# Attention through 32 packed rows, then a squared-ReLU layer: the first batch's second softmax and first layer in two token groups, another order of the transposed keys, one transpose for the left-over tokens, and a new order of the work

## The chip, the cores and the metric

The kernel runs on one core of a Trainium2 chip. The metric is the device time of one execution in microseconds (us). A core has a matrix engine (TensorE, "PE" in the profile; its loads of the stationary operand are listed apart as "PEld"), a vector engine (VectorE, "DVE"), an activation engine (ScalarE, "ACT"), a general engine (GpSimd, "POOL") and an engine that only starts transfers here (SyncE, "SP"). Each engine works off its own queue in the order in which the program put its instructions there; between engines, semaphores make one wait for another. Matrix products land in PSUM, which has eight banks of 512 fp32 values for each of 128 partitions; the other engines read them there and write to SBUF.

## What is computed

```python
def _attn_ref(q, k, v, p):            # q, k, v: 8 batches, 8 heads, 576 tokens, 64; p: 8, 8, 32, 64
    def sm_attn(qq, kk, vv):          # softmax(qq kk^T / 8) vv
        ...
    p_packed = sm_attn(p, k, v)                 # 32 rows for each head: over 576 keys
    return sm_attn(q, p_packed, p_packed)       # 576 rows for each head: over 32 keys

def _moe_ref(x, w_in, w_out):         # x: 4608 tokens x 512, w_in: 512 x 2048, w_out: 2048 x 512
    r = np.maximum(x @ w_in, 0.0)
    return (r * r) @ w_out
```

The first softmax packs each head's keys and values into 32 rows; the second attends from each token to these 32 rows; the heads side by side are x, which goes through two dense layers with a squared ReLU between them. Matrix products run in bf16.

## The kernel before, in words

**Tiles and stages.** The work of a batch b goes through named steps; the names below are those of the code, and the text keeps to them.

- Loads: `Lk`, `Lq` (two each, four heads in one), `Lv` (two), for the weights `LWI` (eight) and `LWO` (eight; number c brings the blocks 2c and 2c+1 of w_out). All are issued on POOL's queue, at most eight unfinished at a time (`dq`), in the order of the list `ld` (lines 790 to 797).
- `Tk`, `Tq` (lines 387 to 396): DVE's 32x32 transposes bring keys and queries into the layout with the head's dimension on the partitions. Row a*18+j of a head lies in partition a, so that the transposed tensor has the order j*32+a.
- `S1` (line 398): scores of the 32 packed rows against 576 keys, two steps for a batch (four heads in each), then maximum (DVE), exponential (ACT) and division (DVE). The values come in another order than the keys, so S1 writes its scores with `main = ps.rearrange("p (g i a j2) -> p i g j2 a")`: neighbouring columns of the product go to every second fp32 value of the PSUM bank. It takes four products of 256 columns and two of 64.
- `E` (line 426): five PE transposes of the weights, and a copy from PSUM. `PV` (line 436): product with the values, 20 small products for each of two steps. `XT`: eight small copies (`pq_block`) and one (`extract`) put the packed rows into `pq_bd` (block diagonal, for S2) and `ppT` (for M).
- `M` (line 464): since x is a product with the packed rows, the first layer's weights are multiplied with them beforehand: M = packed rows times w_in, four chunks of 512 columns.
- `S2` (lines 486 to 535): scores of 576 tokens against 8 x 32 rows. Four token tiles of 128 go into a pair of PSUM banks (16 products), the last 64 tokens into another bank (4 products). DVE takes maximum and difference, ACT the exponential, DVE sum, reciprocal and product. Batch 0 (`SOLO`) does this in three parts (512, 512 and 128 columns), the other batches in one chain `C` of 1152 columns.
- `N` (lines 537 to 549): PE transposes of the result, one step for each half of the heads: four of 128 tokens and, for the last 64 tokens, one whose operand has 64 partitions only (line 544); then one copy of 576 columns.
- `F1` (lines 553 to 579): 16 blocks of 128 of the first layer's 2048 outputs. A step is four products of 288 columns, a ReLU from PSUM into a buffer `r` (four buffers; for batch 0 in two halves that ACT and DVE may share, `SPLIT`), and a square into `gT`, which holds two batches.
- `F2` (lines 583 to 596): for each of 36 tiles of 128 output tokens, 16 products of 512 columns that add up in one PSUM bank, a copy to SBUF and four transfers out on SP's queue. The tiles with even and with odd numbers are two streams, each with one of two banks at a time. Step F2.t.fb needs block fb of the batches that the tile's tokens come from: tiles 0 to 3 lie in batch 0, tile 4 in batches 0 and 1.

**Order.** The program is written by a planner (`Plan`, lines 50 to 227): every step has engines, estimated durations, dependences, PSUM banks and buffers; a list schedule with priorities (`TABLE`, line 230, and `levels`) decides in which order the instructions go into each engine's queue, and which of two engines takes a piece with alternatives. The order is fixed when the program is built. In the first 70 us of the plan, where the planner expects PE to be idle by over 0.45 us, it puts products of a zero matrix ahead of the next step (`keep_clock`, line 302, and `fills`, line 220); they keep PE's clock up and compute nothing.

Of the kernel before, what the change touches and what calls it, by code (L numbers as in the profile page):

```python
# [14 lines left out]
P = 128  # L15
# [34 lines left out]
class Plan:  # L50
# [179 lines left out]
TABLE = {'o': {'X.0': 10.65, 'X.1': 31.58, 'S1.5': 9.41, 'S1.3': -12.52, 'S1.6': -24.93, 'F1.5': 1.74, 'F2.11': 5.6,  # L230
    'N.0': -2.17, 'N.1': -5.48, 'N.2': -15.81, 'N.3': -0.5, 'N.4': -3.15, 'N.5': 4.81, 'N.6': 5.79, 'N.7': 3.42,
    'XT.7': -5.75, 'E.0': 1.99, 'E.1': 1.31, 'E.2': -4.89, 'E.3': -1.37, 'E.4': -8.69, 'E.5': 7.0, 'E.6': 13.74,
    'E.7': 23.02, 'F1.0': -1.88, 'F1.1': -3.45, 'F1.2': -8.22, 'F1.3': -8.4, 'F1.4': -16.3, 'F1.6': 2.12, 'F1.7':
    -14.31, 'P.0': -2.78, 'PV.1': 0.87, 'Tk.5': 8.92, 'M.3': -7.32, 'S1.1': -12.25, 'F2.14': -6.87, 'Tk.3': -0.35,
    'Tq.3': 4.31, 'PV.3': -9.68, 'XT.3': 1.16, 'S2.3': -17.72, 'C.3': -1.2, 'Tk.6': 6.64, 'Tq.6': 46.24, 'PV.6':
    -6.38, 'XT.6': 0.8, 'M.6': 28.77, 'S2.6': -11.88, 'C.6': 19.91, 'XT.4': -14.43, 'I2': -11.49, 'F2.28': 16.93,
    'F2.23': -1.98, 'C.4': -17.29, 'XT.1': -8.34, 'Tq.7': 23.72, 'PV.0': -7.15, 'PV.2': 10.69, 'PV.4': -27.42, 'PV.5':
    -11.67, 'PV.7': 3.53, 'P.2': -15.62, 'XT.5': -13.02, 'M.0': 10.82, 'M.1': 4.52, 'M.2': 10.51, 'M.4': 2.36, 'M.5':
    21.31, 'M.7': 25.09, 'Tk.7': 3.83, 'S1.7': -6.54, 'S2.7': -10.25, 'C.7': 22.2, 'Tq.2': 3.39, 'C.2': -42.42,
    'Tk.4': 26.02, 'Tq.4': 10.05, 'S1.4': -17.0, 'S2.4': -24.58, 'F2.0': 15.91, 'F2.2': -4.29, 'F2.4': 10.23, 'F2.6':  # L240
    6.49, 'F2.8': 8.81, 'F2.10': 12.87, 'F2.12': 20.48, 'F2.16': -1.8, 'F2.18': -3.93, 'F2.20': 10.23, 'F2.22': 6.86,
    'F2.24': 10.11, 'F2.26': 5.69, 'F2.30': 4.43, 'F2.32': -10.27, 'F2.34': 3.66, 'F2.1': 29.8, 'F2.3': 9.19, 'F2.5':
    18.21, 'F2.7': 4.21, 'F2.9': 8.01, 'F2.13': 12.3, 'F2.15': 6.13, 'F2.17': 5.45, 'F2.19': 10.23, 'F2.21': 17.24,
    'F2.25': 7.73, 'F2.27': 6.33, 'F2.29': 7.94, 'F2.31': 6.74, 'F2.33': 14.02, 'F2.35': 19.06, 'Tk.1': -11.46,
    'Tq.1': 1.8, 'S2.1': -26.07, 'C.1': -4.19, 'XT.0': -1.06, 'XT.2': 3.17, 'Tk.2': 0.09, 'S1.2': -4.93, 'S2.2':
    -16.14, 'S2.5': -21.05, 'I': 14.34, 'S2.0': -39.93, 'Tk.0': 0.31, 'Tq.5': 21.62, 'C.5': 7.12, 'S1.0': -9.28,
    'Tq.0': 10.06}, 'l': {'M.0': -0.12, 'M.1': -0.11, 'M.2': -1.84, 'M.3': -0.4, 'M.4': 0.01, 'M.5': -0.79, 'M.6':
    -0.47, 'M.7': -0.5, 'F2.0': -1.53, 'F2.2': -1.2, 'F2.4': -0.22, 'F2.6': -0.74, 'F2.8': -0.4, 'F2.10': -1.53,
    'F2.12': -0.34, 'F2.14': 0.35, 'F2.16': 0.07, 'F2.18': -0.4, 'F2.20': -1.37, 'F2.22': -0.4, 'F2.24': -0.77,
    'F2.26': -1.27, 'F2.28': 0.83, 'F2.30': 0.34, 'F2.32': -0.28, 'F2.34': 1.29, 'F2.1': -0.39, 'F2.3': -0.26, 'F2.5':  # L250
    -0.4, 'F2.7': -0.19, 'F2.9': -0.4, 'F2.11': -0.11, 'F2.13': -3.08, 'F2.15': -0.18, 'F2.17': 0.97, 'F2.19': -0.4,
    'F2.21': -0.4, 'F2.23': 0.97, 'F2.25': 1.65, 'F2.27': -0.4, 'F2.29': -0.4, 'F2.31': -0.8, 'F2.33': 0.25, 'F2.35':
    -0.4, 'E.0': -0.9, 'N.0': 0.35, 'E.5': 1.01, 'XT.3': -0.99, 'N.2': -0.01, 'X.1': 0.09, 'E.7': -1.48, 'N.3': 1.83,
    'E.4': 0.32, 'XT.2': -0.61, 'N.4': 0.55, 'N.6': 0.47, 'N.5': -0.66, 'N.7': 0.73, 'X.0': 0.28, 'XT.5': -1.4,
    'XT.6': 0.52, 'E.1': 0.07, 'XT.1': -0.36, 'XT.7': 0.93, 'E.3': 0.02, 'E.2': -0.51}, 'w': 0, 'm': 1.42}


def kernel_impl(tc, q, k, v, p, w_in, w_out, out):
# [11 lines left out]
    NKQ, NV = 16, 5  # L270
    VX = JT // 2

    with ExitStack() as ctx:
# [6 lines left out]
        rpool = ctx.enter_context(tc.tile_pool(name="rpool", bufs=4))  # L280
# [95 lines left out]
        class Att:  # L376
# [16 lines left out]
            def tr_k(self, qd):  # L393
                nc.vector.transpose(  # L394
                    kT[:, qd].rearrange("p dh (j a) -> p j dh a", a=32),
                    self.t.k[qd][:].rearrange("p (j dh dl) -> p j dh dl", dh=2, dl=32))

            def s1(self, qd, u):
                ps = self.ps1[qd] = pair(u).rearrange("p c n -> p (c n)")[:, :S]
                kv = [kT[:, qd, dh].rearrange("p (j2 x a) -> p x j2 a", j2=2, a=32) for dh in range(2)]  # L400
                w = [pT_bd[:, self.b, qd, dh] for dh in range(2)]
                main = ps[:, :GM * P].rearrange("p (g i a j2) -> p i g j2 a", i=2, a=32, j2=2)
                rest = ps[:, GM * P:].rearrange("p (a j2) -> p j2 a", j2=2)
                for i in range(2):
                    for dh in range(2):
                        nc.tensor.matmul(main[:, i], lhsT=w[dh], rhs=kv[dh][:, i * GM:(i + 1) * GM],  # L406
                                         start=(dh == 0), stop=(dh == 1))
                for dh in range(2):
                    nc.tensor.matmul(rest, lhsT=w[dh], rhs=kv[dh][:, 2 * GM], start=(dh == 0), stop=(dh == 1))  # L409
# [84 lines left out]

            def s2_rest(self, u):
# [6 lines left out]
            def src2(self, x):  # L502
                s = self.ps2r if x == 2 else self.ps2[:, x] if x < 2 else self.ps2[:].rearrange("p c n -> p (c n)")
                return s.rearrange("p (g i) -> p g i", i=32)
# [32 lines left out]
            def s2_tr(self, qd, u):  # L537
                ps = self.pst[qd] = bank(u).bitcast(BF16)[:, :S]
                for tt in range(4):
                    g0 = tt * 8 + qd * QH  # L540
                    nc.tensor.transpose(ps[:, tt * P:(tt + 1) * P],  # L541
                                        self.n2[:, g0:g0 + QH].rearrange("p g i -> p (g i)"), ident[:])
                o = 64 * qd
                nc.tensor.transpose(ps[:, 4 * P:S], self.n2[o:o + 64, 32:36].rearrange("p g i -> p (g i)"),
                                    ident[o:o + 64, o:o + 64])

            def s2_out(self, qd, eng):
                self.tile_of("a2", att, [P, NQD, S], BF16)
                cast(eng, self.a2[:, qd], self.pst[qd])
# [11 lines left out]
        def new_r(a, fb):  # L561
            rr[a.b, fb] = Att.cols(rpool.tile([P, S], BF16, name="r"))
# [38 lines left out]
        OB = [(6,), (7,)]  # L601

        plan = Plan({"kqb": NKQ, "vb": NV, "r": 4, "osb": 3, "dq": 8}, 8)
# [5 lines left out]

        def gate(b, x):  # L610
            y = (b - 2) * NFB + GATE[x] if b > 1 else GATE1[x] if b else -1
            return [f"F1.{y // NFB}.{y % NFB}"] if y >= 0 else []
# [243 lines left out]
```

## Time and profile before

| | us |
|---|---|
| median of 3 runs | 284.8 |
| the three runs | 284.8, 284.81, 282.79 |
| the profiled execution | 282.2 |
| its span, first to last instruction | 280.4 |
| PE busy (of it the zero products of line 304) | 265.5 (21.2) |
| DVE busy | 195.7 |
| ACT busy | 162.2 |
| POOL busy | 46.4 |
| TensorE clock granted | 1.00 throughout |

How to read it: the profiled execution's own time is 1.8 us longer than its span. Busy times of PE count a product from its start to its modelled end, and products overlap, so the mean duration of one (380 ns for 512 columns) is longer than its distance to the next (about 216 ns). What a product costs in a row of products is read from the distance of starts in the timeline. Rows of the timeline merge like instructions: start, time from the first start to the last end, engine, line, operation, operands, shape, number, and in brackets the idle time before and what ended it.

### The profile page before, as it was taken

What the parts mean: (1) busy time and instruction counts of PE and PEld (TensorE: products, weight loads), DVE (VectorE), ACT (ScalarE), POOL (GpSimd) and SP (SyncE); (2) the same over time, 40 slices, a digit from 0 to 9 for tenths busy, and PEclk for the clock granted to TensorE, in tenths of its full rate; (3) what the DMA queues carried; (4) which work ended last, traced back from release to release, by engine and by line L of the source; (5) the groups of instructions that cost most, each with busy time, mean ns of one, the idle gap of its engine ahead of it and who ended that gap; (6) DMA issues with size and microseconds to landing.
All of it is one profiled execution on the core that took longest, in us unless ns stands there. A gap on an engine that the chain in (4) does not pass through costs nothing.

```text
span 280.4 us, 5691 instructions
## 1 busy us (share of the span) xinstructions
PE 265.5 (95%) x2240; PEld 157.9 (56%) x2240; DVE 195.7 (70%) x349; ACT 162.2 (58%) x316; POOL 46.4 (17%) x76
## 2 busy tenths in 40 slices
PE   8976998899999999999999999999999999999992
PEld 6755665445654664666535665464654565356540
DVE  6764687997799658896798678766887644736310
ACT  1453584895856667676455845665645773547500
POOL 8559544343311300000000000000000000000000
PEclk9999999999999999999999999999999999999999
DMA  7999999999999971011122012111112011211132
GB/s 117 200 202 206 203 205 199 206 217 236 218 219 219 173 163 30 12 37 50 29 54 61 2 48 65 42 40 36 40 35 58 25 44 51 58 39 40 27 85 75
DMA packets 26426, 28.48 MB, mean 102 GB/s; under 512 B 5408, under 2 KB 17696, under 8 KB 26400
## 3 DMA queue, kind: packets, MB, share of 16 engines
q0 software_dynamic: 18960, 18.55, 40.5%
q1 hardware_dynamic: 6912, 9.45, 12.4%
q8 instruction: 17, 0.28, 0.4%
q10 hardware_dynamic: 528, 0.13, 0.2%
q14 instruction: 9, 0.07, 0.1%
HBM read 37.22 MB, written 9.44 MB: 166 GB/s over the span
## 4 chain that ended last, share of the span: by engine, by line
PE 88%; DVE 5%; ACT 5%; issue 1%; ACTq 0%; DVEq 0%
PE pb L587 43%; PE ps L557 21%; PE ps L406 5%; PE ps L304 4%; PE ps L492 3%; PE pb L304 2%; PE ps L471 2%; PE pb L444 2%; PE pb L541 2%; PE pb L471 1%; ACT r L569 1%; PE pb L430 1%; ACT M L322 1%; DVE qT L389 1%; DVE pq_bd L324 1%
## 5 line engine op out<-in xcount | busy, mean ns | idle before, releaser
L587 PE MATMUL pb<-w_out_b,gT 128*128 128x512 bf16 x576 | 144.2, 380 | 1.0 <-ACT gT L577 1.0
L569 ACT ACTIVATE r<-ps 128x576 bf16<-128x576 f32 (+1 forms) x127 | 72.9, 609 | 46.8 <-PE ps L557 44.9
L587 PEld LDWEIGHTS <-gT 128*128 128x128 bf16 x576 | 54.1, 99 | 53.7 <-issue 4.2
L557 PE MATMUL ps<-a,M 128*128 128x288 bf16 x512 | 78.7, 286 | 0.4 <-ACT r L569 0.2
L579 DVE TENSOR_TENSOR gT<-r 128x576 bf16<-128x576 bf16 x120 | 53.1, 453 | 24.4 <-ACT r L569 21.8
L557 PEld LDWEIGHTS <-M 128*128 128x128 bf16 x512 | 48.6, 98 | 24.8 <-issue 1.4
L322 ACT COPY o_sb<-pb 128x512 f32<-128x512 f32 x27 | 15.8, 586 | 23.9 <-PE pb L587 23.8
L394 DVE STREAM_TRANSPOSE kT<-k_b 128x1152 bf16<-128x1152 bf16 x16 | 21.6, 1364 | 1.1 <-DMA k_b<-in_k_dram 1.1
L304 PEld LDWEIGHTS <-zero 128*128 128x128 bf16 x160 | 16.1, 103 | 11.1 <-issue 7.2
L389 DVE STREAM_TRANSPOSE qT<-q_b 128x1152 bf16<-128x1152 bf16 x16 | 21.5, 1361 | 0.0
L417 ACT ACTIVATE e1x<-ps,n 128x576 bf16<-128x576 f32 x16 | 11.9, 742 | 14.5 <-DVE n L413 14.5
L322 ACT CAST M<-pb 128x512 bf16<-128x512 f32 x26 | 14.6, 594 | 5.1 <-PE pb L471 5.1
L413 DVE TENSOR_REDUCE n<-ps 128x1 f32<-128x576 f32 x16 | 12.0, 752 | 7.3 <-PE ps L409 7.1
L406 PE MATMUL ps<-kT,pT_bd 128*128 128x256 bf16 x64 | 16.4, 411 | 0.0
L322 ACT CAST M<-ps 128x1024 bf16<-128x1024 f32 x13 | 13.1, 1009 | 5.4 <-PE ps L471 5.3
L304 PE MATMUL ps<-zero 128*128 128x256 bf16 x90 | 12.6, 297 | 3.1 <-ACT r L569 2.0
L324 DVE COPY o_sb<-pb 128x512 f32<-128x512 f32 x9 | 6.2, 691 | 11.8 <-DMA out_dram<-o_sb 8.3
L322 ACT CAST pq_bd<-pb 32x64 bf16<-32x64 f32 x52 | 10.5, 203 | 6.6 <-DVE pq_bd L324 4.4
L522 ACT ACTIVATE e<-d 128x1152 bf16<-128x1152 f32 (+2 forms) x10 | 9.7, 969 | 6.4 <-DVE d L516 6.4
L511 DVE TENSOR_REDUCE m<-ps 128x32 f32<-128x1024 f32 (+1 forms) x9 | 9.9, 1101 | 4.4 <-PE ps L492 4.2
L366 POOL DMA_DIRECT2D v_b<-in_v_dram x16 | 11.2, 707 | 9.8 <-DMA k_b<-in_k_dram 8.4
L304 PE MATMUL pb<-zero 128*128 128x256 bf16 x70 | 8.6, 273 | 4.2 <-ACT M L322 2.1
(61 smaller groups left out, 235.7 us busy)
## 6 DMA issues: line engine op xcount, KB each, us to landing
out_dram<-o_sb SPq DMA_DIRECT2D x144, 64.0 KB, 1.7
k_b<-in_k_dram POOLq DMA_DIRECT2D x16, 288.0 KB, 11.0
q_b<-in_q_dram POOLq DMA_DIRECT2D x16, 288.0 KB, 10.9
v_b<-in_v_dram POOLq DMA_DIRECT2D x8, 320.0 KB, 11.0
v_b<-in_v_dram POOLq DMA_DIRECT2D x8, 256.0 KB, 10.5
w_in_b<-in_moe_w_in_dram POOLq DMA_DIRECT2D x8, 256.0 KB, 10.7
w_out_b<-in_moe_w_out_dram POOLq DMA_DIRECT2D x8, 256.0 KB, 10.3
p_b<-in_p_dram POOLq DMA_DIRECT2D x1, 192.0 KB, 10.5
```

Of the source, the lines that this page charges most:

```text
L304: nc.tensor.matmul(t, lhsT=zero[:, :P], rhs=zero, start=True, stop=True)
L322: nc.scalar.copy(dst, src)
L366: nc.gpsimd.dma_start(self.v[64 * i:64 * i + 64, :, :n * D], src[:, :, i * GM * D:(i * GM + n) * D])
L389: nc.vector.transpose(self.qT[:, qd].rearrange("p dh (j a) -> p j dh a", a=32), self.t.q[qd][:].rearrange("p (j dh dl) -> p j dh dl", dh=2 ...
L394: nc.vector.transpose(kT[:, qd].rearrange("p dh (j a) -> p j dh a", a=32), self.t.k[qd][:].rearrange("p (j dh dl) -> p j dh dl", dh=2, dl=32))
L406: nc.tensor.matmul(main[:, i], lhsT=w[dh], rhs=kv[dh][:, i * GM:(i + 1) * GM], start=(dh == 0), stop=(dh == 1))
L413: nc.vector.tensor_reduce(self.n1[:, qd:qd + 1], self.ps1[qd], axis=AX.X, op=ALU.max, negate=True)
L417: nc.scalar.activation(e1x[:, qd], self.ps1[qd], ACT.Exp, bias=self.n1[:, qd:qd + 1], accum_out=self.d1[:, qd:qd + 1])
L557: nc.tensor.matmul(ps[:, c], lhsT=a.M[:, qd, fb * FB:(fb + 1) * FB], rhs=a.a2[:, qd, c * HALF:(c + 1) * HALF], start=(qd == 0), stop=(qd = ...
L569: nc.scalar.activation(dst, src, ACT.Relu)
L579: eng.tensor_tensor(out=Att.cols(gT[:, fb, o:o + S]), in0=r, in1=r, op=ALU.mult)
L587: nc.tensor.matmul(po[t], lhsT=gT[:, fb, n0:n0 + P], rhs=w_out_b[:, fb, :], start=(fb == 0), stop=(fb == NFB - 1))
```

## The change

It has six parts.

1. Keys: the transpose `tr_k` writes the order that S1 wants (every second value of kT), and S1 reads kT in sequence, in two products of 512 columns and two of 64, written in runs of 64 fp32 values.
2. Left-over tokens: N is cut by tokens instead of by heads (`s2_trh`, `s2_outh`): step x=0 has four transposes (tokens 0 to 255), step x=1 four (256 to 511) and one of 128 partitions for the last 64 tokens of all heads, written as 2 x 64 columns; the copies have 512 and 640 columns.
3. Batch 0: S2 goes into single banks by token halves (`s2_half`), step N.0.0 follows the first half's chain, and the first layer runs as `FA.0.j` (tokens 0 to 255) and `F1.0.j` (tokens 256 to 575), each step two blocks of 128 outputs (four products of 256 or 320 columns), with one ReLU and one square for both. The tiles 0 and 1 of F2 need FA alone.
4. M of batch 0 may use the bank pairs of F1 too (`MB0`); there are six buffers r instead of four, each of 640 columns.
5. Loads: batch 1's keys are issued ahead of LWO 2 and 3, and the fills of constants on POOL (`setup2`) stand after batch 1's values instead of before its keys.
6. A new `TABLE` of priorities (and wait and margin of the planner), so a new order on all engines. The built program has 122 zero products instead of 160; ahead of S1 of batch 0 there are 44 in both.

```diff
             def tr_k(self, qd):
                 nc.vector.transpose(
-                    kT[:, qd].rearrange("p dh (j a) -> p j dh a", a=32),
-                    self.t.k[qd][:].rearrange("p (j dh dl) -> p j dh dl", dh=2, dl=32))
+                    kT[:, qd].rearrange("p dh (x a j2) -> p j2 x dh a", a=32, j2=2),
+                    self.t.k[qd][:].rearrange("p (j2 x dh dl) -> p j2 x dh dl", j2=2, dh=2, dl=32))
 
             def s1(self, qd, u):
                 ps = self.ps1[qd] = pair(u).rearrange("p c n -> p (c n)")[:, :S]
-                kv = [kT[:, qd, dh].rearrange("p (j2 x a) -> p x j2 a", j2=2, a=32) for dh in range(2)]
                 w = [pT_bd[:, self.b, qd, dh] for dh in range(2)]
-                main = ps[:, :GM * P].rearrange("p (g i a j2) -> p i g j2 a", i=2, a=32, j2=2)
-                rest = ps[:, GM * P:].rearrange("p (a j2) -> p j2 a", j2=2)
-                for i in range(2):
-                    for dh in range(2):
-                        nc.tensor.matmul(main[:, i], lhsT=w[dh], rhs=kv[dh][:, i * GM:(i + 1) * GM],
-                                         start=(dh == 0), stop=(dh == 1))
+                main = ps[:, :GM * P].rearrange("p (g i n) -> p i g n", i=2, n=64)
                 for dh in range(2):
-                    nc.tensor.matmul(rest, lhsT=w[dh], rhs=kv[dh][:, 2 * GM], start=(dh == 0), stop=(dh == 1))
+                    nc.tensor.matmul(main, lhsT=w[dh], rhs=kT[:, qd, dh, :GM * P], start=(dh == 0), stop=(dh == 1))
+                for dh in range(2):
+                    nc.tensor.matmul(ps[:, GM * P:], lhsT=w[dh], rhs=kT[:, qd, dh, GM * P:], start=(dh == 0), stop=(dh == 1))
...
+            def s2_half(self, x, u):
+                if x == 0:
+                    self.ps2h = {}
+                t = self.ps2h[x] = bank(u)
+                for tt in range(2 * x, 2 * x + 2):
+                    for qd in range(NQD):
+                        c0 = (tt % 2) * 2 * P + qd * P
+                        for dh in range(2):
+                            nc.tensor.matmul(t[:, c0:c0 + P], lhsT=self.qT[:, qd, dh, tt * P:(tt + 1) * P],
+                                             rhs=self.pq_of(qd, dh), start=(dh == 0), stop=(dh == 1))
...
-            def s2_tr(self, qd, u):
-                ps = self.pst[qd] = bank(u).bitcast(BF16)[:, :S]
-                for tt in range(4):
-                    g0 = tt * 8 + qd * QH
-                    nc.tensor.transpose(ps[:, tt * P:(tt + 1) * P],
-                                        self.n2[:, g0:g0 + QH].rearrange("p g i -> p (g i)"), ident[:])
-                o = 64 * qd
-                nc.tensor.transpose(ps[:, 4 * P:S], self.n2[o:o + 64, 32:36].rearrange("p g i -> p (g i)"),
-                                    ident[o:o + 64, o:o + 64])
...
+            def s2_trh(self, x, u):
+                n = TOKH[x]
+                ps = self.pst[x] = bank(u).bitcast(BF16)[:, :NQD * n]
+                for qd in range(NQD):
+                    for tt in range(2 * x, 2 * x + 2):
+                        g0, c0 = tt * 8 + qd * QH, qd * n + (tt - 2 * x) * P
+                        nc.tensor.transpose(ps[:, c0:c0 + P], self.n2[:, g0:g0 + QH].rearrange("p g i -> p (g i)"), ident[:])
+                if x:
+                    nc.tensor.transpose(ps.rearrange("p (q n) -> p q n", q=NQD)[:, :, 2 * P:],
+                                        self.n2[:, 32:36].rearrange("p g i -> p (g i)"), ident[:])
...
+        def fh_mm(a, x, j, u):
+            ps = ph[x, j] = pair(u)[:, :, :TOKH[x]]
+            o = x * 2 * P
+            for e in range(2):
+                fb = 2 * j + e
+                for qd in range(NQD):
+                    nc.tensor.matmul(ps[:, e], lhsT=a.M[:, qd, fb * FB:(fb + 1) * FB], rhs=a.a2[:, qd, o:o + TOKH[x]],
+                                     start=(qd == 0), stop=(qd == NQD - 1))
...
+            def deps(fb):
+                return [f"FA.0.{fb // 2}"] if t < 2 else [f1n(b, fb) for b in bs]
...
+        ORDER = ("k0 v0 q0 i0 a0 a1 a2 a3 b0 b1 k1 b2 b3 v1 i1 b4 b5 q1 b6 b7 p2 "
+                 + " ".join(f"k{b} v{b} q{b}" for b in range(2, B)))
```

## The prediction

> **What bounds the kernel now.** I read the page first (busy shares), then the busy time by stretches of the span, then PE's timeline, then the issues on POOL's queue.
>
> ```profile
> PE 265.5 (95%) x2240; PEld 157.9 (56%) x2240; DVE 195.7 (70%) x349; ACT 162.2 (58%) x316; POOL 46.4 (17%) x76
> ```
>
> The stretches with the zero products alone (line 304; columns: stretch, length, PE busy, PE weight loads, clock, DMA share, GB/s):
>
> ```profile
> 7.40:60.00 52.60, 14.87 (x118) 11.06 (x116) 1.00 1.25 204
> 60.00:275.40 215.40, 0.00 (x0) 0.00 (x0) 1.00 0.36 77
> ```
>
> PE is the bound from 60 us to the last product at 275.4 us; before 60 us it fills its waits with zero products while the loads come in. So the busy share hides a weak head. How long each kind of work takes PE in a row is the distance of starts in the timeline:
>
> ```profile
> 70.23 0.44 PE L430 MATMUL pb<-ident,e1n 128*128 128x128 bf16 x5
> 70.51 0.65 PE L557 MATMUL ps<-a,M 128*128 128x288 bf16 x4
> 71.00 0.38 PE L587 MATMUL pb<-w_out_b,gT 128*128 128x512 bf16 x1
> 71.22 0.65 PE L557 MATMUL ps<-a,M 128*128 128x288 bf16 x4
> ...
> 85.12 1.03 PE L406 MATMUL ps<-kT,pT_bd 128*128 128x256 bf16 x4
> 85.94 0.32 PE L409 MATMUL ps<-kT,pT_bd 128*128 128x64 bf16 x2
> 86.06 1.49 PE L587 MATMUL pb<-w_out_b,gT 128*128 128x512 bf16 x6
> ...
> 92.48 0.39 PE L541 MATMUL pb<-ident,n 128*128 128x128 bf16 x4
> 92.80 0.20 PE L544 MATMUL pb<-ident,n 64*128 64x64 bf16 x1
> 92.93 0.40 PE L541 MATMUL pb<-ident,n 128*128 128x128 bf16 x4
> 93.26 0.20 PE L544 MATMUL pb<-ident,n 64*128 64x64 bf16 x1
> 93.39 0.82 PE L587 MATMUL pb<-w_out_b,gT 128*128 128x512 bf16 x3
> ```
>
> Five transposes take 0.28, so 0.056 each; an F1 step 0.49; an F2 product of 512 columns 0.216. The four S1 products of only 256 columns take 0.82, hardly less than four of 512: they run at half rate, and these are the ones that write every second PSUM value. One S1 step takes 0.94 (85.12 to 86.06). N takes 0.91 (92.48 to 93.39): its ten transposes would take 0.56 at 0.056, so each 64-partition one costs about 0.18 more, in the distance ahead of it and behind it.
>
> PE's useful work in these distances: F2 576 x 0.2167 = 124.8, F1 128 x 0.49 = 62.7, S1 16 x 0.94 = 15.0, S2 8 x 1.22 = 9.8, E 4.5, PV 6.9, N 8 x 0.91 = 7.3, M 9.0: 240.0 us. PE starts useful work at 7.4 and ends at 275.4: 268.0, so 28 us are waits or zero products. Up to the first F1 product of batch 1, at 59.94, it has done 28.8 (all of S1, E, PV, S2, M and N of batches 0 and 1, all F1 of batch 0, 36 F2), so 23.7 of the 28 lie in the head and 4.3 behind.
>
> ```profile
> 45.48 1.58 PE L304 MATMUL ps<-zero 128*128 128x256 bf16 x13 [1.29 <-ACT r L569]
> 46.89 1.06 PE L492 MATMUL ps<-pq_bd,qT 128*128 128x128 bf16 x16
> ...
> 59.94 0.66 PE L557 MATMUL ps<-a,M 128*128 128x288 bf16 x4
> ```
>
> What the head could reach is set by the loads. An issue on POOL waits for the landing of the load eight issues earlier, so the bracket dates that landing:
>
> ```profile
> 40.87 0.56 POOL L361 DMA_DIRECT2D q_b<-in_q_dram  x1 [0.71 <-DMA q_b<-in_q_dram]
> 42.18 0.55 POOL L361 DMA_DIRECT2D q_b<-in_q_dram  x1 [0.74 <-DMA w_out_b<-in_moe_w_out_dram]
> ```
>
> The second half of batch 1's queries lands just before 40.9 and LWO 6 just before 42.2, 1.3 us for each load, LWO 7 as much later. Yet S2 of batch 1 starts at 46.89 only.
>
> **S1, the strided keys.** Columns stay the same. Two products of 512 columns at 0.216 and two of 64, which took 0.06 each and can take 0.03: 0.49 to 0.55, I take 0.53, 0.41 less. Ends: 0 if the half rate has another cause (the products then take 0.43 each), 0.45 at best; a loss is excluded, as nothing is longer and two weight loads go. Sum 16 x 0.41 = 6.6 us of PE.
>
> **The transposes that write it.** Line 394 writes runs of 32 values now; in the new kernel it writes every second bf16 value. The count stays, and no row shows such a write.
>
> ```profile
> L394 DVE STREAM_TRANSPOSE kT<-k_b 128x1152 bf16<-128x1152 bf16 x16 | 21.6, 1364 | 1.1 <-DMA k_b<-in_k_dram 1.1
> L389 DVE STREAM_TRANSPOSE qT<-q_b 128x1152 bf16<-128x1152 bf16 x16 | 21.5, 1361 | 0.0
> ```
>
> Lower end 1.36 (a gain is excluded: same count, no simpler order). Upper end 2.7, by the S1 products, whose stepped writes halve the rate. I take 1.36, since 1152 elements in 1.36 us is a stream of one element after the other, with a step of 4 bytes where S1's was 8. The Trainium skill (SBUF — State Buffer, section "Door 1: The DMA port swizzle") says that SBUF works in lines of 16 bytes and needs two hits in a line, and PSUM in lines of 8 bytes: by that rule four bf16 values at this step share a line and the transposes cost nothing more, where the S1 row's doubling would add 21.8 us to DVE. No run here shows it yet.
>
> **N.** Nine transposes of 128 partitions: 9 x 0.056 = 0.50, 0.41 less; ends 0.35 (the 2 x 64 write at half rate) to 0.91 (nothing gained). 8 x 0.41 = 3.2 us. The copies move the same columns (0.46 us of DVE each before), on either engine. F1 of batch 0 has the same columns (16 x 4 x 288 = 8 x 4 x (256 + 320)): 0. Its ReLUs and squares become 32 instructions instead of 48 on ACT and DVE; that counts in the head only.
>
> **The head.** I followed the new order by hand, with the durations of these rows and the landings above. Batch 0: keys transposed by 8.6, both S1 steps in PE by 9.25 (before 9.9), E copies now on DVE, PV done 13.3 (before 14.2), but its queries land at 13.4 and need two transposes: S2 at 15.65 (before 15.83). First half's chain on DVE: maxima and differences of both halves to 18.95, sums, reciprocals and the first product to 21.5. PE is by then behind M's third chunk, which waits for w_in, and seven zero products: N.0.0 at 22.9 (before 28.64). FA from 23.85 (before F1 from 30.0), with F2 of tiles 0 and 1 behind the LWO loads. LWO 2 and 3 now land behind batch 1's keys, some 2.8 us later (31.0 and 32.3): PE waits there for w_out in between, but also has S1 of batch 1 earlier (30.65 against 35.5). S2 of batch 1 needs the second transposed queries: landing 40.6, the DVE behind two squares, 42.75. So S2 at 42.8, 4.1 earlier. Behind it PE has F2 (38 products, 8.2 us), two F1 steps, M and the last S2 piece until N.1 at 52.4; DVE's chain (1.22 + 1.21 + 0.28 x 2, exponential 1.16, 1.34 + 0.38 + 1.35 and what stands between) ends at 52.1. The copies stand behind a key transpose of 1.36 and end at 54.4.
>
> So F1 of batch 1 starts at 54.45 instead of 59.94, with 64 F2 done instead of 36. Useful work by then, at the new prices: S1 2.1, E 1.1, PV 1.7, S2 2.4, M 2.2, N 1.0, F1 7.8, F2 64 x 0.2167 = 13.9: 32.3. Lost in the head: 54.45 - 7.4 - 32.3 = 14.7, against 23.7: 9.0 us gained. Ends: 0 (the waits come back elsewhere) to 11.
>
> Moved on POOL: `setup2` (2.7 + 1.9 us) now stands ahead of LWO 4 to 7 and batch 1's queries. Six loads of 1.3 us are then under way, and LWO 4, issued at about 30.2, is due at 36.5 only: hidden; without that cover up to 4.6 us at S2 of batch 1. PV.1 needs its values' zeros by 36.4, they are there at 30.2. The four copies that spread the later packed rows go from ACT (0.84 each) to DVE between F1 squares, due at 65: hidden.
>
> **Behind the head.** 240.0 - 9.8 - 32.3 = 197.9 us of PE work remain. The waits there were 4.3. Per batch PE needs 28.8 instead of 30, DVE still about 24 and ACT 21, so there is less to hide behind; and in F1 of batch 1 all 16 ReLUs (0.65 each) are now ACT's, behind two output copies of 0.59. I take 5.8, near the row; bounds 4.3, and 4.3 + 6 x 1.2 = 11.5 if what PE saves in each of six batches becomes a wait for DVE or ACT. Last product: 54.45 + 197.9 + 5.8 = 258.1; the tail (copy and transfers, 275.45 to 280.4) stays 4.95: span 263.1, own time 264.9 against 282.2, 17.3 less. The median of the runs stands 2.6 above the profiled one, so on that scale **267 us**.
>
> The change has fewer zero products (78 instead of 116 behind the first S1). The longest wait of PE now is 2.08 us, with the clock at 1.00 in every stretch; the longest in my walk is 1.7, so I count no cost. The Trainium skill (TensorE: Matmul & The Clock Gate, section "Why this matters for your kernels") asks for no idle gap over about 3 us; by it a gap that grew that far would halve the clock for some 3.4 us, an estimate of 1.7 us lost.
>
> **Rivals.**
> - Head half lost: DVE or ACT, in order, let S2.1 and N.1 slip (for it: DVE is at 9.5 of 10 us busy in 50 to 60 already). 267 + 4.5 to 267 + 9: 271.5 to 276. Chance 0.12; with still more waits behind it, up to 287, no change: 0.03.
> - S1 stays at half rate: 267 + 6.6 = 273.6. For it: only one form is in the trace. Against: F2 writes in sequence at full rate. 0.06.
> - Key transposes take 2.7: head 2.7 later, and DVE some 26.7 of 28.8 us per batch, about 0.7 of wait in each of six: 267 + 7 = 274. 0.06.
> - Slower than before: key transposes at over about 5 us each. DVE has 149 us of work in the 200 us from 60 to 260; thirteen transposes with 3.7 more fill 197 of them, so each wait of DVE, 25% of its time now, delays the end; with 5% of them (11) and a head some 10 later 267 becomes 288. Below about 4.5 us each it stays faster. 0.04.
> - Better: S1 at its best and waits as before, 259 to 262: 0.06.
> - The forecast, own range 262 to 271: 0.63.
>
> **Numbers.** A measurement of this kernel tells about 1% from no change. Faster by over 1% (below 282): 0.63 + 0.06 + 0.12 + 0.06 + 0.06 = 0.93; within 1% 0.03; slower 0.04. The range, with the first three rivals, is 260 to 276.
>
> **What would show it.** S1 products of 512 columns 0.216 apart; line 396's transposes at 1.36 us; nine N transposes in 0.50; S2 of batch 1 near 42.8, F1 of batch 1 near 54.5; PE gapless from there. Wrong would be: 0.43 between S1 products, transposes over 2 us, or a busy PE that only starts at 60 us again.

## The result and the profile after

| | before | after |
|---|---|---|
| median, us | 284.81 (282.79 to 284.81, 4 runs) | 263.07 (262.55 to 264.31, 4 runs) |
| ratio, 95% interval | | 0.926 (0.921 to 0.931) |
| profiled execution, its span, us | 282.2, 280.4 | 262.87, 261.0 |
| F1 of batch 1 starts, us | 59.94 (36 F2 products done) | 54.43 (64 done) |
| last product of PE ends, us | 275.4 | 255.84 |

The predicted 267 was 4 us too high, inside its range. The page's first part, of the kernel after:

```profile
PE 250.4 (96%) x2162; PEld 145.5 (56%) x2162; DVE 196.7 (75%) x343; ACT 162.5 (62%) x306; POOL 46.3 (18%) x76
```

PE works 15.1 us less in a span 19.4 us shorter; DVE's work is the same as before, 1 us aside, in less time. So PE is still the bound, and the missing part of the gain (19.4 - 15.1 = 4.3 us) is idle time of PE, the start and the tail included. The stretches with the zero products alone (line 306), columns as in the prediction:

```profile
7.40:54.43 47.03, 10.22 (x80) 7.18 (x78) 1.00 1.25 209
54.43:255.84 201.41, 0.00 (x0) 0.00 (x0) 1.00 0.42 87
```

Zero products are down from 14.87 to 10.22 us of busy time, and the clock is 1.00 in both stretches. PE's timeline of the kernel after, around the places that the prediction dates:

```profile
13.23 0.49 PE L442 MATMUL pb<-e,v_b 128*64 128x32 bf16 x20
15.81 2.12 PE L306 MATMUL pb<-zero 128*128 128x256 bf16 x18 [2.09 <-ACT ppT L324]
17.77 1.06 PE L501 MATMUL pb<-pq_bd,qT 128*128 128x128 bf16 x16
...
23.50 0.40 PE L552 MATMUL pb<-ident,n 128*128 128x128 bf16 x4
...
24.42 1.03 PE L580 MATMUL ps<-a,M 128*128 128x256 bf16 x8
...
42.32 0.59 PE L623 MATMUL pb<-w_out_b,gT 128*128 128x512 bf16 x2 [0.37 <-DMA w_out_b<-in_moe_w_out_dram]
42.75 1.05 PE L490 MATMUL ps<-pq_bd,qT 128*128 128x128 bf16 x16
...
52.42 0.61 PE L552 MATMUL pb<-ident,n 128*128 128x128 bf16 x8
52.87 0.22 PE L554 MATMUL pb<-ident,n 128*128 128x128 bf16 x1
52.92 1.68 PE L623 MATMUL pb<-w_out_b,gT 128*128 128x512 bf16 x7
54.43 1.14 PE L567 MATMUL ps<-a,M 128*128 128x288 bf16 x8
...
65.80 0.60 PE L405 MATMUL ps<-kT,pT_bd 128*128 128x512 bf16 x2
66.23 0.22 PE L407 MATMUL ps<-kT,pT_bd 128*128 128x64 bf16 x2
66.29 0.38 PE L623 MATMUL pb<-w_out_b,gT 128*128 128x512 bf16 x1
```

One S1 step takes 66.29 - 65.80 = 0.49 us (before 0.94), its 512-column products 0.216 each and its 64-column products 0.03 each. N takes 52.92 - 52.42 = 0.50 for both halves together (before 0.91). S2 of batch 1 starts at 42.75 (before 46.89). S2 of batch 0 starts at 17.77 (before 15.83): later, with no harm to what follows.

DVE's transposes of the kernel after, grouped by line:

```profile
L396 DVE STREAM_TRANSPOSE kT<-k_b 128x1152 bf16<-128x1152 bf16 x16 | 22.8, 1452 | 1.3 <-DMA k_b<-in_k_dram 1.2
L391 DVE STREAM_TRANSPOSE qT<-q_b 128x1152 bf16<-128x1152 bf16 x16 | 21.6, 1364 | 0.1
```

The keys' transpose, which now writes every second value, takes 1452 ns where the queries' one, unchanged, takes 1364: 6% more, not twice as much. Two dates of DVE in the timeline bear on the head, the transposes of batch 1's queries and the copies of its N:

```profile
39.57 2.79 DVE L391 STREAM_TRANSPOSE qT<-q_b 128x1152 bf16<-128x1152 bf16 x2
53.21 0.78 DVE L326 COPY a<-pb 128x512 bf16<-128x512 bf16 x2
```

The queries are ready at 42.36, 0.39 us before S2 of batch 1 starts, and the copies are done at 53.99, 0.44 us before its F1. PE was what both starts waited for: two F2 products stand ahead of S2 and wait until 42.32 for their block of w_out, and from there PE works without a wait to F1. POOL's issues, whose brackets date the landings:

```profile
41.24 0.56 POOL L363 DMA_DIRECT2D q_b<-in_q_dram  x1 [0.72 <-DMA q_b<-in_q_dram]
42.56 0.55 POOL L363 DMA_DIRECT2D q_b<-in_q_dram  x1 [0.76 <-DMA w_out_b<-in_moe_w_out_dram]
```

The second half of batch 1's queries lands just before 41.2 (before 40.9), LWO 6 just before 42.6 (before 42.2). The loads come at the same pace as before; PE now uses them earlier. All waits of PE that semaphores ended, in the kernel after (us in total, times, longest):

```profile
PE pb L306 <- ACT ppT L324: 2.1, 1, 2.1
PE ps L306 <- DVE zero L329: 1.1, 1, 1.1
PE ps L567 <- ACT r L605: 0.8, 3, 0.3
PE pb L623 <- DMA w_out_b<-in_moe_w_out_dram: 0.4, 1, 0.4
PE ps L405 <- DVE kT L396: 0.2, 1, 0.2
PE ps L306 <- ACT M L324: 0.2, 1, 0.2
```

Behind 54.43 us only the third row is left: F1 waiting for ACT's ReLUs, 0.8 us in all.

### The profile page after: what moved, and what is told of

Its sections match the earlier page's. It is cut to its first block, busy times and chain, and to the rows that moved or that the text cites. A ratio compares the mean times of both kernels' runs of the same rounds, so it can differ in the third digit from the quotient of the medians.

```text
span 261.0 us, 5504 instructions
## 1 busy us (share of the span) xinstructions
PE 250.4 (96%) x2162; PEld 145.5 (56%) x2162; DVE 196.7 (75%) x343; ACT 162.5 (62%) x306; POOL 46.3 (18%) x76
## 4 chain that ended last, share of the span: by engine, by line
PE 73%; DMA 13%; POOL 4%; SPq 3%; ACT 3%; issue 1%; DVE 1%; ACTq 0%; POOLq 0%
PE pb L623 40%; PE ps L567 20%; DMA w_in_b<-in_moe_w_in_dram 4%; DMA w_out_b<-in_moe_w_out_dram 4%; DMA q_b<-in_q_dram 3%; SPq L632 3%; PE ps L490 3%; PE ps L405 2%; DMA out_dram<-o_sb 2%; PE pb L442 2%; PE ps L469 2%; ACT r L605 1%; PE pb L428 1%; PE pb L469 1%; POOL pT_bd L336 1%
## 5 line engine op out<-in xcount | busy, mean ns | idle before, releaser
L623 PE MATMUL pb<-w_out_b,gT 128*128 128x512 bf16 x576 | 148.1, 380 | 0.5 <-DMA w_out_b<-in_moe_w_out_dram 0.4
L605 ACT ACTIVATE r<-ps 128x576 bf16<-128x576 f32 x112 | 71.7, 651 | 20.6 <-PE ps L567 15.9
L567 PE MATMUL ps<-a,M 128*128 128x288 bf16 x448 | 72.0, 286 | 0.9 <-ACT r L605 0.8
L615 DVE TENSOR_TENSOR gT<-r 128x576 bf16<-128x576 bf16 x112 | 49.9, 455 | 26.8 <-ACT r L605 25.7
L567 PEld LDWEIGHTS <-M 128*128 128x128 bf16 x448 | 43.0, 98 | 24.4 <-issue 3.4
L396 DVE STREAM_TRANSPOSE kT<-k_b 128x1152 bf16<-128x1152 bf16 x16 | 22.8, 1452 | 1.3 <-DMA k_b<-in_k_dram 1.2
L391 DVE STREAM_TRANSPOSE qT<-q_b 128x1152 bf16<-128x1152 bf16 x16 | 21.6, 1364 | 0.1
L324 ACT CAST M<-ps 128x1024 bf16<-128x1024 f32 (+1 forms) x17 | 14.3, 860 | 3.8 <-PE ps L469 3.8
L306 PEld LDWEIGHTS <-zero 128*128 128x128 bf16 x122 | 12.2, 104 | 6.3 <-issue 2.9
L324 ACT CAST pq_bd<-pb 32x64 bf16<-32x64 f32 x52 | 10.5, 202 | 8.3 <-PE pb L442 7.4
L324 ACT CAST M<-pb 128x512 bf16<-128x512 f32 x25 | 13.9, 599 | 1.4 <-PE pb L469 1.3
L368 POOL DMA_DIRECT2D v_b<-in_v_dram x16 | 11.2, 699 | 12.7 <-DMA k_b<-in_k_dram 4.9
L306 PE MATMUL ps<-zero 128*128 128x256 bf16 x79 | 11.2, 301 | 1.3 <-DVE zero L329 1.1
L537 DVE TENSOR_REDUCE t<-e 128x36 f32<-128x1152 bf16 (+2 forms) x10 | 11.0, 1096 | 1.5 <-ACT e L531 1.2
L363 POOL DMA_DIRECT2D k_b<-in_k_dram x16 | 8.7, 542 | 14.1 <-DMA q_b<-in_q_dram 3.7
L363 POOL DMA_DIRECT2D q_b<-in_q_dram x16 | 9.0, 565 | 12.5 <-DMA v_b<-in_v_dram 6.3
## 6 DMA issues: line engine op xcount, KB each, us to landing
w_in_b<-in_moe_w_in_dram POOLq DMA_DIRECT2D x8, 256.0 KB, 11.2
p_b<-in_p_dram POOLq DMA_DIRECT2D x1, 192.0 KB, 10.5
```

Of the source, the lines that this page charges most:

```text
L306: nc.tensor.matmul(t, lhsT=zero[:, :P], rhs=zero, start=True, stop=True)
L324: nc.scalar.copy(dst, src)
L363: nc.gpsimd.dma_start(t, src[self.b, qd * QH:(qd + 1) * QH].rearrange("h (a j) d -> (h a) (j d)", j=JT))
L368: nc.gpsimd.dma_start(self.v[64 * i:64 * i + 64, :, :n * D], src[:, :, i * GM * D:(i * GM + n) * D])
L391: nc.vector.transpose(self.qT[:, qd].rearrange("p dh (j a) -> p j dh a", a=32), self.t.q[qd][:].rearrange("p (j dh dl) -> p j dh dl", dh=2 ...
L396: nc.vector.transpose(kT[:, qd].rearrange("p dh (x a j2) -> p j2 x dh a", a=32, j2=2), self.t.k[qd][:].rearrange("p (j2 x dh dl) -> p j2 x ...
```

## Experiments

Theory on going in: the gain has three sources that hardly touch each other, S1's products (7.2 us), N's (3.3 us) and a head with 9 us less of waits and zero products. The rivals doubted each of them. Unless a diff says otherwise, a kernel is the changed one. Dates are those of each kernel's profiled execution. "Head loss" below is the time of zero products plus the excess of each distance of starts over the usual distance of its kind, from 7.3 to 75 us: 26.4 us before, 17.0 after.

### The keys as before (old_keys)

```diff
-                    kT[:, qd].rearrange("p dh (x a j2) -> p j2 x dh a", a=32, j2=2),
+                    kT[:, qd].rearrange("p dh (j a) -> p j dh a", a=32),
...
-                main = ps[:, :GM * P].rearrange("p (g i n) -> p i g n", i=2, n=64)
+                main = ps[:, :GM * P].rearrange("p (g i a j2) -> p i g j2 a", i=2, a=32, j2=2)
...
```

> The changed kernel with part 1 undone: keys transposed in the old order, S1 with strided writes, all else and the order of all instructions as in the changed kernel. Theory (PE is the bound behind the head, so its work counts in full): an S1 step goes from 0.49 back to 0.94 us; 12 steps behind the head cost 5.4, the four in the head 0 to 1.8: 268.5 to 270.3 where the changed kernel takes 263.1 and the kernel before 284.8. Rival (DVE and ACT are close to the bound behind the head, and PE's saving turns into waits for them): under 265.5.

Measured: 271.32 us (269.6 to 271.58), 0.9545 (0.949 to 0.960) of before. Head loss 16.4. So part 1 is worth 8.2 us by the medians, 1.0 beyond the expected range, where 7.2 are PE's own time. The profiled executions, at clock 1.00 up to the last product in both, differ by 269.6 - 262.87 = 6.7; the other four of this kernel took 270.8 to 271.58 at mean clocks of 0.990 to 0.993, so the excess goes with the clock (last section). The S1 step is back at its old price:

```profile
112.48 1.04 PE L408 MATMUL ps<-kT,pT_bd 128*128 128x256 bf16 x4
113.31 0.32 PE L411 MATMUL ps<-kT,pT_bd 128*128 128x64 bf16 x2
```

Four products of 256 columns take 113.31 - 112.48 = 0.83 us. The gain is where the prediction put it.

### Which side is slow, the read or the write (read_stepped, write_stepped)

Before, S1 both read the keys with a jump and wrote every second PSUM value. Each kernel keeps one of the two.

```diff
 read_stepped:
...
-                main = ps[:, :GM * P].rearrange("p (g i n) -> p i g n", i=2, n=64)
+                for i in range(2):
+                    for dh in range(2):
+                        nc.tensor.matmul(ps[:, i * 2 * P:(i + 1) * 2 * P], lhsT=w[dh], rhs=kv[dh][:, i * GM:(i + 1) * GM],
+                                         start=(dh == 0), stop=(dh == 1))
...
 write_stepped:
...
+                        nc.tensor.matmul(main[:, i], lhsT=w[dh], rhs=kT[:, qd, dh, i * 2 * P:(i + 1) * 2 * P],
+                                         start=(dh == 0), stop=(dh == 1))
...
```

> The changed kernel with the keys transposed in the old order and S1 reading them in runs of 32 with a jump, as in the kernel before, but writing PSUM in sequence, in four products of 256 columns; the scores then stand in another order than the values, which changes the result. Theory (writing every second PSUM value is what halves S1's rate): the products are 0.11 us apart. Rival (reading in short runs is): 0.20 to 0.22 as before.

> The changed kernel with the key transposes of before; S1 reads 256 keys in sequence in each product (no jump) and writes every second PSUM value as before. It pairs scores with the wrong keys, so the result is changed: it is for the distance of its products. By the theory that the stepped PSUM write sets the half rate: 215 ns between products of 256 columns, as before and as in old_keys, one run at 268 to 272. Rival, that the read in runs of 32 did: 108 ns and about 264.

Measured, one run each: 263.81 us with the read in jumps, 271.4 us with the stepped write. PE's timeline of the first:

```profile
66.74 0.60 PE L406 MATMUL ps<-kT,pT_bd 128*128 128x256 bf16 x4
67.18 0.22 PE L409 MATMUL ps<-kT,pT_bd 128*128 128x64 bf16 x2
```

and of the second:

```profile
114.28 1.04 PE L407 MATMUL ps<-kT,pT_bd 128*128 128x256 bf16 x4
115.11 0.32 PE L410 MATMUL ps<-kT,pT_bd 128*128 128x64 bf16 x2
```

The same four products take 0.44 us with the read in jumps (109 ns apart) and 0.83 with the stepped write (216 ns apart). So the stepped PSUM write set the half rate. The prediction gave that from a single form; here it is separated.

### The left-over tokens by heads (rest_by_heads)

Batches 1 to 7 have N by heads again, with two transposes of 64 partitions.

```diff
-                return Step(nn, [[[("PE", 0.24 + 0.06 * x, lambda: T[b].s2_trh(x, U[nn]))]],
+                return Step(nn, [[[("PE", 0.24 + 0.06 * x, lambda: (T[b].s2_trh if b in SOLO else T[b].s2_tr)(x, U[nn]))]],
...
```

> The changed kernel with part 2 undone for batches 1 to 7: N by heads, with two transposes of 64 partitions each; batch 0 keeps the token halves. Theory: N goes from 0.50 back to 0.91 us, 7 x 0.41 = 2.9, all of it on PE's path: 265.5 to 266.1. Rival (hidden by waits for DVE and ACT): 263.1 to 264.

Measured: 266.52 us (265.89 to 267.13), 0.938 (0.933 to 0.943). 3.4 us for seven batches, 0.3 beyond what was expected at most. The timeline of this kernel:

```profile
85.49 0.39 PE L565 MATMUL pb<-ident,n 128*128 128x128 bf16 x4
85.81 0.20 PE L568 MATMUL pb<-ident,n 64*128 64x64 bf16 x1
85.94 0.40 PE L565 MATMUL pb<-ident,n 128*128 128x128 bf16 x4
```

Four transposes at 0.056 would end at 85.71; the fifth starts at 85.81, and the next ones 0.13 behind it. This accounts for 7 x 0.41 = 2.9 of the 3.4 us. The profiled executions differ by 265.89 - 262.87 = 3.0; the rest lies within the spread of the executions.

### Parts 1 and 2 alone, in the kernel before (before_keys_rest)

The kernel before with parts 1 and 2 of the change and nothing else; part 1's diff stands above with the signs turned round, part 2 is this:

```diff
-                res.append(Step(nn, [[[("PE", 0.45, lambda qd=qd, nn=nn: T[b].s2_tr(qd, U[nn]))]],
+                res.append(Step(nn, [[[("PE", 0.45, lambda qd=qd, nn=nn: T[b].s2_trh(qd, U[nn]))]],
...
```

> The kernel before with parts 1 and 2 alone (keys' order, N by token groups with one transpose for the rest), with its own order, loads and first layer. Theory: behind its head PE saves 12 x 0.45 + 6 x 0.41 = 7.9 us, in the head 0 to 2.6 of it: 274.3 to 276.9 against 284.8; the other 11 to 14 us of the change are the head's. Rival 1 (the old order cannot use a shorter PE queue): over 280. Rival 2 (shorter S1 and N are what shortens the head too): under 271.

Measured: 274.27 us (273.78 to 275.41), 0.966 (0.961 to 0.971). So 10.4 us by the medians come from the two parts that only cheapen PE's work, and 282.42 - 273.78 = 8.6 by the fastest executions of both; PE's own saving is 16 x 0.45 + 8 x 0.41 = 10.5. From F1 of batch 1 to its last product PE takes 207.2 us instead of 215.4: 8.2 less, where 7.9 were expected. That F1 starts at 61.33 (before 59.94), and the head loss is 30.3 us. In this execution 1.7 of it is the clock: it stood at half from 21.91 to 25.33, and 19 zero products there took 3.83 us instead of 2.16. Without that F1 would start some 0.3 us earlier than before: of the 2.6 us that are cheaper in the head, most turns into waits there. The other 11.2 us belong to the cut of batch 0, the loads and the table.

### The loads as before (old_loads)

Parts 1 to 4 and 6 stay; the queue of POOL alone is put back.

```diff
+LATER = ["LWO.2", "LWO.3", "I2", "Lk.1.0", "Lk.1.1", "Lv.1.0", "Lv.1.1"]
...
```

> The changed kernel with part 5 undone in POOL's queue alone: LWO 2 and 3 and the constants ahead of batch 1's keys, as in the kernel before; every other queue unchanged. Theory (S2 of batch 1 waits for its queries, which land at the same time): S1 of batch 1 starts some 2.5 us later, S2 of batch 1 at 43 to 44 us instead of 42.75, time 263.1 to 264.6. Rival (the early keys make the head's gain): S2 of batch 1 at 45 us or later, time 266 or more.

Measured: 264.67 us (264.29 to 266.11), 0.9325 (0.928 to 0.9375); S2 of batch 1 at 44.21 instead of 42.75, F1 of batch 1 at 55.89 instead of 54.43. Both slip by the same 1.46 us, and the end by 1.6, each just beyond what was expected. The slip starts at S1 of batch 1: PE waits 2.26 us there for the transposed keys, until 32.38 (30.22 in the kernel after), and has no wait from there to S2 of batch 1, where the kernel after waits 0.37 for w_out. So it isn't the queries that carry it. Part 5 is worth little, and it is the earlier keys.

### The wait ahead of S2 of batch 0 (zero_free, no_zero18)

In the kernel after, 18 zero products stand ahead of S2.0. They write the bank that PV's result was copied from, so they wait for that copy (ppT); S2.0 stands behind them. zero_free sends them to a bank that is free; no_zero18 leaves them out.

```diff
 zero_free:
+                if x == 0:
+                    keep_clock(ps[0][:, 0, :2 * P])
 no_zero18:
+                plan.fill = 0
```

> The changed kernel with the 18 zero products ahead of S2 of batch 0 written to a PSUM bank that is free, so that they run during the wait for ppT instead of behind it. Theory (until some 42 us the loads of w_in, w_out and the queries set the pace, and PE's waits there cost nothing): S2 of batch 0 at 15.8 us instead of 17.8, N.0.0 still behind w_in at 23.2 to 23.5, F1 of batch 1 at 54.0 to 54.5, time within 0.6 us of the changed kernel's 263.1. Rival (the batch 0 chain sets the head's length): F1 of batch 1 at 53 or earlier, 261 to 261.6.

> The changed kernel without the 18 zero products ahead of S2 of batch 0: PE then waits in one gap from about 13.7 to about 16.5 us for that step. By the walk of the head the end doesn't move: S2.0 at 16 to 16.6, N.0.0 at 23.0 to 23.5, F1 of batch 1 at 54.4 to 54.6, 262.5 to 264. If a gap of over 2 us can trip the clock, a stretch of about 3.4 us at granted clock 0.50 follows in some executions, for up to 2 us: runs then between 262.5 and 265.5. If the zero products are what holds the clock, every execution is 2 us longer: 265.

Measured: zero_free 262.98 us (262.88 to 263.14), 0.924 (0.921 to 0.927), with S2.0 at 16.51 and F1 of batch 1 at 54.48; no_zero18 263.11 (262.87 to 263.64), 0.928 (0.924 to 0.933), with S2.0 at 16.91, N.0.0 at 25.06 and F1 of batch 1 at 55.28. Neither moves the median by more than 0.1 us. S2.0 of zero_free came 0.7 us later than expected, in an execution whose first S1 starts 1.1 us later than in the kernel after (8.78 against 7.67), and N.0.0 at 23.00, 0.2 earlier. What this gains is gone at 42.37, where PE waits 0.54 us for w_out: up to there the loads set the pace. The dates of no_zero18, later than expected, are of an execution with 6.8 us at half clock: its 16 products of S2.0 take 1.80 us instead of 0.99. S2.0's late start costs nothing, and without the 18 zero products not every execution is 2 us longer, as the last of the expectations had it. What the clock did is in the last section.

### Batch 0's first layer in one piece (halves_undone)

```diff
-            if b in SOLO:
-                return fh_steps(0) + fh_steps(1)
...
-                return [f"FA.0.{fb // 2}"] if t < 2 else [f1n(b, fb) for b in bs]
+                return [f1n(b, fb) for b in bs]
...
```

The priority of F1.0 takes FA's place in the table; the second softmax keeps its two halves.

> The changed kernel with the first layer of batch 0 in 16 steps over all 576 tokens, as in the kernel before (S2 and N by halves stay, F2 needs those steps, priority that of FA); the planner orders anew, the queues are the same up to N.0.0. Theory (S2 of batch 1 is set by the landing of its queries and of w_out, the halves only give PE work earlier): F1 of batch 0 starts some 4 us later, S2 of batch 1 at 44 to 45 us instead of 42.75, F1 of batch 1 at 56 to 58, time 265 to 267. Rival (the halves make the head's gain of 9 us): F1 of batch 1 at 60 or later, 269 or more.

Measured: 277.01 us (276.76 to 277.36), 0.9736 (0.970 to 0.977). My theory fell: I had held that the cut is worth little beside the order, and taking it away cost 13.9 us. PE's timeline of this kernel:

```profile
16.04 3.73 PE L306 MATMUL pb<-zero 128*128 128x256 bf16 x18 [2.09 <-ACT ppT L324]
...
26.66 1.27 PE L306 MATMUL pb<-zero 128*128 128x256 bf16 x10
27.76 0.39 PE L552 MATMUL pb<-ident,n 128*128 128x128 bf16 x4
27.99 0.22 PE L554 MATMUL pb<-ident,n 128*128 128x128 bf16 x1
28.08 0.60 PE L306 MATMUL ps<-zero 128*128 128x256 bf16 x4
28.79 1.14 PE L567 MATMUL ps<-a,M 128*128 128x288 bf16 x8
```

F1 of batch 0 now needs both halves of N and starts at 28.79 instead of 24.42, with zero products in between. Then S2 of batch 1 comes at 48.97 (42.75) and F1 of batch 1 at 62.09 (54.43): a loss of 4.4 us at the start has grown to 7.7. Not all of the 4.4 is the cut's: the 18 zero products ahead of S2.0 ran at half clock (3.57 us to the next start, 1.96 in the kernel after), so N.0.0 came 1.8 us late already, at 25.32. And 6.3 of the 13.9 us are lost behind F1 of batch 1, from where PE takes 269.78 - 62.09 = 207.7 us to its last product instead of 201.4, with a wait of 1.9 for DVE at 98 among others. The planner also put other steps late (PV of batch 1 at 46.54), under priorities that suit the cut; this kernel cannot tell the two apart.

### The table of before, with and without that cut (old_table, old_table_no_fa)

The first has parts 1 to 5 and before's `TABLE`; the second also takes out the cut of the first layer, by the diff above.

```diff
-TABLE = {'o': {'F2.10': 9.46, 'Tk.7': 21.4, 'Tq.7': 33.99, 'S1.7': 1.48, 'E.7': 32.14, 'PV.7': 37.91, 'XT.7': 25.64,
...
+TABLE = {'o': {'X.0': 10.65, 'X.1': 31.58, 'S1.5': 9.41, 'S1.3': -12.52, 'S1.6': -24.93, 'F1.5': 1.74, 'F2.11': 5.6,
...
```

> The changed kernel with the kernel before's table of priorities: parts 1 to 5 without part 6; the planner orders anew everywhere. Theory (the early first layer, the loads and PE's shorter work make the gain, not the priorities): F1 of batch 1 at 54 to 57 us, 264 to 268. Rival (the new order makes it): 270 or more.

> The changed kernel with the table of priorities of before and with batch 0's first layer in 16 steps over all 576 tokens (parts 1, 2, 4, 5 and the cut of the second softmax; parts 6 and the cut of the first layer undone; replanned). Beside old_table (270.13 us, F1 of batch 1 at 62.3) it differs by the cut of the first layer alone, under priorities that were not made for it. Theory: the cut itself brings the head forward, since F1 of batch 0 then waits for the whole second softmax: 3 to 6 us over old_table, 273 to 276, first F1 step of batch 0 at 27 to 29 instead of about 24. Rival: the 13.9 us that halves_undone lost came from priorities that were made for the cut, and the cut is worth nothing under others: 269 to 271.5.

Measured: old_table 270.13 us (269.49 to 271.06), 0.949 (0.946 to 0.953); old_table_no_fa 271.98 (271.64 to 272.3), 0.960 (0.956 to 0.964). Timelines, first the one with the cut:

```profile
26.20 0.60 PE L579 MATMUL ps<-a,M 128*128 128x256 bf16 x4
27.69 0.38 PE L305 MATMUL ps<-zero 128*128 128x256 bf16 x2 [0.89 <-DVE M L325]
27.91 1.03 PE L579 MATMUL ps<-a,M 128*128 128x256 bf16 x8
```

and without it:

```profile
26.40 2.57 PE L305 MATMUL pb<-zero 128*128 128x256 bf16 x22
...
30.11 1.14 PE L566 MATMUL ps<-a,M 128*128 128x288 bf16 x8
```

The cut brings batch 0's first layer forward by 3.9 us here (26.20 against 30.11), fills the 22 zero products' place with work, and takes head loss from 27.2 to 24.8. F1 of batch 1 starts at 62.34 with it and at 61.87 without, but with 64 F2 products done against 49, which is 3.2 us of PE's work; the last product ends at 262.67 and 265.48. So the old priorities pass 2.8 of the 3.9 us on in these executions, 1.9 by the medians. The 1.9 us lie between what theory and rival expected; neither was right. With the cut, the new table is worth 270.13 - 263.07 = 7.1 us; without it, it loses 277.01 - 271.98 = 5.0, up to 1.7 of which can be the half clock of halves_undone. So cut and table are one part in truth: singly they bring 1.9 and -5.0, together 8.9.

## Why the prediction was right, point by point

The runs that add parts one after the other make a sum (each term good to 1 to 2 us, as the runs lie on several chips and some executions lose about 2 us to the clock): parts 1 and 2 take 284.8 to 274.3; N and S2 of batch 0 by halves with parts 4 and 5, to 272.0; the first layer's cut, to 270.1; the table, to 263.1. Other orders of adding give other shares for the last three.

- **S1.** Mechanism right. The two 64-column products take 0.03 each, the end that the prediction left open and did not take: 0.49 a step and not 0.53. 16 x 0.04 = 0.6 us too little.
- **Key transposes.** 1452 ns, near the lower end (1.36) as chosen. DVE's 1.4 us more cost PE one wait of 0.2 us. The Trainium skill's rule (SBUF — State Buffer, section "Door 1: The DMA port swizzle") led to the right side against the doubling of the S1 row; that it costs nothing is not quite borne out: 6%.
- **N.** 0.50, as predicted.
- **The head.** F1 of batch 1 at 54.43 (predicted 54.45), with 64 F2 done; N.1 at 52.42 (52.4), S2 of batch 1 at 42.75 (42.8), the first FA step at 24.42 (23.85). By the prediction's own prices the head loses 54.43 - 7.4 - 32.1 = 14.9 us, against 14.7. One step of the walk failed: "S2 at 15.65". I took PE to fill that time with zero products, and did not see that these wait for a PSUM bank; S2.0 stood behind them until 17.77. It cost almost nothing: in zero_free S2.0 comes 1.26 us earlier, PE then waits 0.46 us for w_in in M instead, and N.0.0 comes only 0.5 us earlier (23.00), F1 of batch 1 not at all. Two dates were right for another reason than the walk's, and that is luck. The walk let S2 of batch 1 wait for its queries until 42.75; they were ready at 42.36, and w_out with two F2 products held it until 42.75. It let F1 of batch 1 wait for copies that end at 54.4; they ended at 53.99, and PE's own queue set 54.43. With PE's work between the two dates as counted, the head came out at its length.
- **Loads.** LWO 4 came at 36.9 (36.5 predicted), `setup2` stayed hidden.
- **Behind the head.** "I take 5.8" was too much. By the same prices, 255.84 - 54.43 = 201.4 us hold 197.4 of work (S1 at 0.49) and 4.0 of waits, less than the 4.3 of before by that account. Counted from the distances themselves, waits are 1.1 us before and 2.1 after: the "4.3" was largely the error of rounded prices over 200 us. The cover did get thinner, as said, and it cost 1 us.
- **The scale.** 264.9 for the profiled execution became 267 by adding the 2.6 us that the median before stood above its profiled run; the sum is 267.5. After, that distance is 0.2. Carrying it over was half of the miss: of 267.5 - 263.07 = 4.4 us, 2.0 are 262.87 against 264.9 (waits 1.8, S1 0.5, the tail 0.25 the other way), and 2.4 are this.
- **Rivals.** The half-lost head did not come: DVE is at 75%, and PE waits for it behind the head nowhere. S1 at half rate, key transposes at 2.7 or over 5 us: excluded by the rows above. The nearest was "better, 259 to 262", which missed by 1 us.

What stays open: which of the table's entries carry the 7.1 us, and whether a table made for the uncut first layer would come nearer. That wasn't tried.

## What to carry to other kernels

What this kernel showed can be tried elsewhere. When PE is the bound, look at the distance of starts of each form of product, not at its busy time: a product at half rate shows there, and its destination's step is the first suspect. Work that becomes cheaper ahead of the first saturated stretch turns into waits; there, ask what the next stretch's first operand needs and cut that into a piece that can go early, and change the order with it, for a cut without its order (1.9 us) or an order without its cut (-5.0) shows little of what both bring (8.9). Do not take a small difference of two large rounded sums for waits: count the excess of each distance instead.

## What the runs showed of the hardware that was not expected

**A gap of 2.1 us can be enough for half clock.** In the prediction I counted no cost for a wait of about 2 us of PE. In the profiles of before and after such a wait passed at clock 1.00. In the profile of rest_by_heads, the same wait (from 13.25 us, ended by ppT at 15.35) did not. Columns: stretch, length, busy time of PE, PEld, DVE, ACT and POOL, PE clock, DMA share, GB/s:

```profile
14.00:15.00 1.00, 0.00 (x0) 0.00 (x0) 1.00 (x1) 0.95 (x5) 0.47 (x1) 0.94 1.25 206
15.00:16.00 1.00, 0.65 (x4) 0.45 (x4) 0.25 (x1) 0.27 (x2) 0.72 (x1) 0.50 1.29 220
16.00:17.00 1.00, 1.00 (x6) 0.68 (x5) 0.00 (x0) 0.00 (x0) 0.66 (x1) 0.50 1.17 186
17.00:18.00 1.00, 1.00 (x7) 0.72 (x5) 0.00 (x0) 0.00 (x0) 0.05 (x1) 0.50 1.25 202
18.00:19.00 1.00, 1.00 (x12) 0.82 (x11) 0.00 (x0) 0.00 (x0) 0.56 (x1) 0.86 1.25 206
```

About 3.4 us at 0.50, starting before PE has gone to work again. before_keys_rest, halves_undone, read_stepped and write_stepped show stretches of the same length, each at one such gap; no_zero18, behind a gap of 2.10 us, shows twice that, from about 16.2 to 23.0:

```profile
16.00:17.00 1.00, 0.09 (x2) 0.09 (x2) 0.81 (x1) 0.81 (x4) 0.44 (x2) 0.61 1.24 204
17.00:18.00 1.00, 1.00 (x11) 1.00 (x11) 0.00 (x0) 0.00 (x0) 0.68 (x1) 0.50 1.30 220
...
22.00:23.00 1.00, 1.00 (x7) 0.70 (x5) 0.96 (x4) 0.49 (x2) 0.72 (x1) 0.50 1.21 200
23.00:24.00 1.00, 1.00 (x17) 0.70 (x15) 0.99 (x2) 0.00 (x0) 0.62 (x1) 0.98 1.26 209
```

The Trainium skill (TensorE: Matmul & The Clock Gate, section "Why this matters for your kernels") asks for no idle gap over about 3 us; here 2.1 us were enough in some executions and not in others with the same gap. The length of the stretch agrees with its 3.4 us. It also says (section "What's actually happening") that this window runs freely and doesn't start with the kernel; that would let the same gap fall differently into it from one execution to the next. The traces agree. In each of the six, the changes of the clock lie whole multiples of 3.413 us apart over the whole execution: in before_keys_rest it fell at 21.91, rose at 25.33 and fell again behind the last product at 271.09, and 271.09 - 25.33 = 245.76 is 72 times 3.413. Counted back from the fall behind the last product, the edges of this window can be placed in the other traces too. In the gap ahead of S2.0 an edge lies 0.82 us behind the gap's start in the kernel after, 0.47 in old_keys and 0.35 in old_loads, and the clock stayed; in the five others it lies 1.40 to 2.13 us behind it, and the clock fell there. In the kernel before, whose gap follows other work, an edge 1.64 us behind its start passed, and in before_keys_rest one at 2.20 did not. So with the same gap the phase decides; what else the rule counts isn't shown.

What it costs depends on what stands there. Of 21 executions of the kernel before beside the experiments, 14 had a mean clock of 0.992 to 0.994 (3.4 us at half clock in 280 make 0.994) and took 284.25 to 285.22 us; the other 7, at 0.995 to 1.000, took 282.42 to 283.22. That is about 2 us, the distance of the median from the profiled run; no profile shows such an execution of the kernel before, so the link goes by the mean clock alone. A fall behind the last product lowers the mean too and costs nothing: halves_undone, with the longest one (3.0 us), loses 0.0055 by it. In no_zero18 an execution at 0.989 took 262.87, one at 1.000 took 263.34, and the profiled one, with 6.8 us at half clock, 263.64: little or no loss, where zero products and waits fill the stretch. zero_free, where PE never waits over 0.54 us once S1 has begun and whose profile shows full clock up to the last product, has the narrowest spread of all kernels with more than one execution, 0.26 us.
